# Moving the bit conversion of the second layer's weights between the experts of a mixture kernel

## The chip, the cores and the metric

The kernel runs on one core of one Trainium2 chip. The metric is the device time of one execution in microseconds (us); smaller is better. The kernel before takes 867.17 us, the median of three runs (866.35 to 868.37).

## The reference

Three stages run one after the other in one launch: attention over 4 batches, 8 heads, 512 local and 32 global positions; a mixture of eight experts in which every token goes to one expert; and a dense layer with a nonlinearity. Cut to the two later stages:

```python
def _moe_ref(x, w_gate, w1, w2):                # x: 2176 tokens x 512
    expert_idx = np.argmax(x @ w_gate, axis=1)
    gate_w = softmax(x @ w_gate)[np.arange(N), expert_idx]
    for e in range(8):
        mask = expert_idx == e
        h = np.maximum(x[mask] @ w1[e], 0.0)    # 512 -> 1024
        out[mask] = gate_w[mask, None] * (h @ w2[e])
def _moe2_ref(x, w_in, w_out):
    h = x @ w_in                                # 512 -> 2048, w_in and w_out are float64
    return (h - np.tanh(h)) @ w_out
```

## The kernel before

**Stages.** Attention and routing take the first 180 us or so. The experts follow, up to about 466 us, and the second layer after that.

**Experts.** Expert 0 comes first, the other seven in an order that the kernel finds from their token counts. The position in this order is called a place here, 0 to 7 (the variable `e` of `expert`, `expert_small`, `ahead`, the variable `p` of `CONV`). The places with more than 128 tokens (in this run 0, 1, 3, 5, 6 and 7) take the function `expert`, in which the tokens are the moving side of the matmuls; places 2 and 4 take `expert_small`. Each place has eight chunks `m` of 128 hidden units.

**Order in a place.** The schedule is written out by hand: each engine runs its instructions in the order of the program. For chunk m, `expert` emits the first matmuls `emit_L1(m)` (L1010, into the PSUM bank `pL1[m % 2]`), the two evictions of that bank (ACT's Relu L1013, DVE's low part L1014), the second matmuls `emit_L2(m - 2)` (L1021), and then `ahead(e, m)`. So TensorE's line reads L1(0), L1(1), L1(2), L2(0), L1(3), L2(1), ... L1(7), L2(5), L2(6), L2(7). A bank of `pL1` comes free when both evictions have read it: L1(m) waits for DVE's L1014 of chunk m - 2.

**What `ahead` emits.** First the split of a later chunk's weights into a high and a low part (ACT L935 twice, DVE L936, POOL L936), then the loads of raw weights on SP's queue (L120, L122), and then the conversion that this change is about.

**Conversion.** `w_in` and `w_out` arrive as float64. DVE builds the float32 bits from pairs of 32-bit words. There are 20 pieces q of 512 KB: 0 to 15 are the column blocks of `w_in`, 16 to 19 the first four row blocks of `w_out`. A piece at chunk m has its first two DVE operations (L946, L949, `pre_conv1`) at the end of `ahead(e, m)`; the third one (L952), ACT's rounding copy (L957), DVE's subtraction (L958) and the load of piece q + 2 (L965 or L968 on SP's queue, `pre_load`) follow in `ahead(e, m + 1)`, ahead of the first two operations of the next piece. The raw words lie in two buffers, `raw64[q % 2]`, so the load of piece q + 2 waits for L952 of piece q, and L946 of piece q waits for the load of piece q. The first two loads are issued ahead of place 0.

```python
        if (e, m - 1) in convs:
            pre_conv2(convs[e, m - 1], tmp64)   # L952, L957, L958, load of piece q + 2
        if (e, m) in convs:
            pre_conv1(convs[e, m], tmp64)       # L946, L949
```

`CONV` lists for each place the chunks that carry a piece, and `convs` numbers the pieces in that order. Before, place 0 has pieces 0, 1, 2 at chunks 0, 2, 4; place 1 has 3 to 9 at chunks 0 to 6; place 3 has 10 to 13 at 0, 1, 3, 4; places 5 and 7 have three each at 0, 2, 4.

Of the kernel before, what the change touches and what calls it, by code (L numbers as in the profile page):

```python
# [46 lines left out]
def body(ctx: ExitStack, tc: tile.TileContext, q_l, k_l, v_l, q_g, k_g, v_g,  # L47
# [980 lines left out]

    LS = 3

    CONV = ((0, 2, 4), (0, 1, 2, 3, 4, 5, 6), (), (0, 1, 3, 4), (), (0, 2, 4), (), (0, 2, 4))
    convs = {pm: q for q, pm in enumerate((p, m) for p in range(E) for m in CONV[p])}


# [440 lines left out]
```

## Time and profile before

| | |
|---|---|
| median of 3 runs | 867.17 us (866.35 to 868.37) |
| profiled execution | 869.88 us, its span 868.2 us |
| mean granted TensorE clock | 0.973 of full speed |
| TensorE (PE) busy | 801.0 us, 92% |
| VectorE (DVE) busy | 670.7 us, 77% |
| ScalarE (ACT) busy | 485.5 us, 56% |
| GpSimd (POOL) busy | 324.5 us, 37% |

The profile comes from one execution. Its own time is 1.68 us above its span (what lies around the first and the last instruction) and 2.71 us above the median of the runs. Times in rows count from the start of the span. In a row of the order in time the columns are start, duration, engine, line, operation, written tile, read tiles, shape and count; the brackets at the end give the idle time just ahead of it on its engine and what ended that. Matmul durations overlap their successors by about 0.16 us, so distances are better read from start to start.

### The profile page before, as it was taken

The numbers are of one execution on the slowest core, as the hardware profiler recorded it, in microseconds if no ns is written. First come the engines' busy times: TensorE is split into PE (matmuls) and PEld (weight loads), VectorE is DVE, ScalarE is ACT, GpSimd is POOL, SyncE is SP. The second block draws the span as 40 slices with busy tenths as digits, with TensorE's granted clock in tenths as the row PEclk, the third lists the DMA queues.
The fourth block names the chain that finished last, engine by engine and source line by source line (L and its number), as shares of the span: only waits on it lengthen the run. The fifth ranks groups of instructions, "written<-read, shape, count | busy, mean of one in ns | idle before, by whom it ended". The sixth has DMA issues, their size and how long they took to land. (4 is left out here: it accounts for less than half of the span.)

```text
span 868.2 us, 16570 instructions
## 1 busy us (share of the span) xinstructions
PE 801.0 (92%) x5456; PEld 698.1 (80%) x5456; DVE 670.7 (77%) x1430; ACT 485.5 (56%) x1179; POOL 324.5 (37%) x405
## 2 busy tenths in 40 slices
PE   8989999969899797787979988999999999999996
PEld 6767777758788687687979877789998999999885
DVE  6879999855468686776466999898698788778784
ACT  5777877634334443444535655575566565566564
POOL 7322253333212334333511566433433433343332
PEclk9999999979989899999989999999999999999999
DMA  6699974253856888798853223000000000010000
GB/s 147 140 251 225 279 195 148 91 192 97 266 168 197 204 237 255 180 264 281 213 130 103 83 91 109 25 24 26 25 22 27 13 35 19 1 44 1 12 26 25
DMA packets 145261, 105.71 MB, mean 122 GB/s; under 512 B 76608, under 2 KB 122176, under 8 KB 145088
## 3 DMA queue, kind: packets, MB, share of 16 engines
q1 hardware_dynamic: 142368, 94.83, 40.7%
q0 software_dynamic: 2720, 8.95, 2.7%
q8 instruction: 63, 1.03, 0.5%
q14 instruction: 110, 0.90, 0.4%
HBM read 78.75 MB, written 25.02 MB: 120 GB/s over the span
## 5 line engine op out<-in xcount | busy, mean ns | idle before, releaser
L1368 POOL TENSOR_TENSOR u<-u,z 128x384 f32<-128x384 f32 (+1 forms) x96 | 122.3, 1274 | 225.1 <-ACT u L1366 213.1
L936 POOL TENSOR_TENSOR w2s<-raw,w2s 128x512 fp32r<-128x512 f32 x64 | 90.4, 1420 | 192.7 <-ACT w2s L935 130.0
L1010 PE MATMUL pL<-xT,w1a 128*128 128x256 f32 (+4 forms) x588 | 110.4, 345 | 12.7 <-issue 4.8
L1010 PEld LDWEIGHTS pL<-xT,w1a 128*128 128x128 f32 x588 | 96.7, 209 | 22.9 <-issue 8.6
L1396 PE MATMUL pL<-wo,gT 128*128 128x512 f32 x417 | 108.9, 394 | 0.0
L1021 PE MATMUL pL<-hT,w2s 128*128 128x256 f32 (+4 forms) x576 | 98.2, 323 | 0.0
L1021 PEld LDWEIGHTS pL<-hT,w2s 128*128 128x128 f32 x576 | 87.2, 189 | 6.5
L1396 PEld LDWEIGHTS pL<-wo,gT 128*128 128x128 f32 x417 | 77.6, 188 | 14.3
L1383 DVE TENSOR_TENSOR gT<-g,gT 128x384 fp32r<-128x384 f32 (+1 forms) x64 | 80.5, 1258 | 0.7 <-ACT gT L1361 0.7
L936 DVE TENSOR_TENSOR w1a<-raw,w1a 128x512 fp32r<-128x512 f32 x64 | 62.6, 982 | 7.1 <-ACT w1a L935 4.2
L365 ACT ACTIVATE P<-sc,mx 128x224 f32<-128x224 f32 x128 | 60.6, 477 | 12.4 <-DVE mx L356 11.9
L1053 PE MATMUL pL<-xT,wih 128*128 128x384 f32 x256 | 65.3, 335 | 1.1 <-PEq L1282 1.1
L1373 DVE TENSOR_TENSOR g<-pL,z 128x384 f32<-128x384 f32 (+1 forms) x64 | 34.0, 531 | 41.5 <-ACT d L1356 41.5
L1355 ACT ACTIVATE z<-pL 128x384 f32<-128x384 f32 (+1 forms) x64 | 30.2, 471 | 61.9 <-PE pL L1053 59.7
L1053 PE MATMUL pL<-yB,wih 128*128 128x384 f32 (+1 forms) x256 | 59.5, 318 | 0.0
L1366 ACT ACTIVATE u<-z,c1t 128x384 f32<-128x384 f32 (+1 forms) x96 | 58.0, 605 | 0.0
L1367 ACT ACTIVATE mk<-z,nth 128x384 bf16<-128x384 f32 (+1 forms) x96 | 56.7, 590 | 0.0
L1379 DVE SCALAR_TENSOR_TENSOR g<-u,g 128x384 f32<-128x384 f32 (+1 forms) x96 | 55.1, 574 | 0.0
L1396 PE MATMUL pL<-wo,xT 128*128 128x512 f32 x207 | 54.5, 395 | 0.1
L1014 DVE SCALAR_TENSOR_TENSOR hT<-pL,hT 128x256 fp32r<-128x256 f32 (+4 forms) x48 | 24.9, 520 | 32.5 <-ACT hT L1013 32.4
L1053 PEld LDWEIGHTS pL<-xT,wih 128*128 128x128 f32 x256 | 46.7, 188 | 3.9 <-issue 1.4
L1361 ACT CAST gT<-g 128x384 fp32r<-128x384 f32 (+1 forms) x64 | 31.8, 496 | 31.8 <-DVE g L1387 31.8
(288 smaller groups left out, 1892.1 us busy)
## 6 DMA issues: line engine op xcount, KB each, us to landing
raw<-in_moe_w_dram SPq DMA_DIRECT2D x128, 256.0 KB, 6.0
xs<-zrow SPq DMA_DIRECT2D x32, 258.0 KB, 4.9
raw<-in_moe_w_in_dram SPq DMA_DIRECT2D x16, 512.0 KB, 5.2
raw<-in_moe_w_out_dram SPq DMA_DIRECT2D x16, 512.0 KB, 3.8
xrow<-xs SPq DMA_DIRECT2D x12, 516.0 KB, 5.7
yc<-yst SPq DMA_DIRECT2D x20, 256.0 KB, 5.7
nk<-in_k_l_dram SPq DMA_DIRECT2D x32, 128.0 KB, 3.7
nq<-in_q_l_dram SPq DMA_DIRECT2D x32, 128.0 KB, 3.4
```

Of the source, the lines that this page charges most:

```text
L365: nc.scalar.activation(out=P[:, j, 0:W], in_=sc[:, j], func=ACTF.Exp, scale=-1.0, bias=mx[:, j:j + 1], accum_out=sums[n][:, 2 * ip + j, h: ...
L936: (nc.gpsimd if lo else nc.vector).tensor_tensor(out=dl, in0=t[:, lo:lo + 512], in1=dh.bitcast(F32), op=ALU.subtract)
L1010: nc.tensor.matmul(ps[:, c], w1s[s][a][:, k], xT[x][:, k, c], start=a + x + k == 0, stop=x == 1 and k == KD - 1)
L1021: nc.tensor.matmul(pL2[j][:, 0:N], w2s[s][a][:, 128 * j:128 * (j + 1)], h[x][:, 0:N], start=st, stop=sp)
L1053: nc.tensor.matmul(ps[:, 0:n], a[:, m, k], y[x][:, k, 0:n], start=st, stop=sp)
L1366: nc.scalar.activation(out=u, in_=z, func=ACTF.Identity, scale=C2, bias=c1t)
L1367: nc.scalar.activation(out=mk, in_=z, func=ACTF.Relu, bias=nth)
L1368: nc.gpsimd.tensor_tensor(out=u, in0=u, in1=z, op=ALU.mult)
L1373: nc.vector.tensor_tensor(out=g, in0=h, in1=z, op=ALU.mult)
L1379: nc.vector.scalar_tensor_tensor(out=g, in0=u, scalar=C0, in1=g, op0=ALU.add, op1=ALU.mult)
L1383: nc.vector.tensor_tensor(out=t[1][:, 0:n], in0=g, in1=t[0][:, 0:n].bitcast(F32), op=ALU.subtract)
L1396: nc.tensor.matmul(p, g[a][:, 128 * j:128 * (j + 1)], w, start=st, stop=sp)
```

## The change

One table is changed. Place 0 gets pieces 0 to 6 at chunks 0 to 6, place 1 gets 7 to 13 at chunks 0 to 6, place 3 gets 14, 15 and 16 at chunks 1, 3 and 5, place 5 gets 17 and 18 at chunks 1 and 4, and place 7 gets 19 at chunk 2. The number of pieces is 20 in both.

```diff
-    CONV = ((0, 2, 4), (0, 1, 2, 3, 4, 5, 6), (), (0, 1, 3, 4), (), (0, 2, 4), (), (0, 2, 4))
+    CONV = (range(7), range(7), (), (1, 3, 5), (), (1, 4), (), (2,))
     convs = {pm: q for q, pm in enumerate((p, m) for p in range(E) for m in CONV[p])}
```

## Rows read from the trace of the kernel before

**Rows 1.** The page, its first part: busy time, share and instructions.

```profile
PE 801.0 (92%) x5456; PEld 698.1 (80%) x5456; DVE 670.7 (77%) x1430; ACT 485.5 (56%) x1179; POOL 324.5 (37%) x405
```

**Rows 2.** Busy time by stretch: length, engines, then clock, DMA share, GB/s. Places 0, 3.

```profile
core 0: us, PE busy (x) PEld busy (x) DVE busy (x) ACT busy (x) POOL busy (x), PEclk, DMA share, GB/s
189.50:233.50 44.00, 43.81 (x204) 38.22 (x204) 20.66 (x29) 15.59 (x29) 12.42 (x9) 0.96 0.62 179
...
312.00:347.50 35.50, 30.27 (x192) 29.42 (x192) 23.90 (x36) 14.69 (x31) 12.75 (x9) 0.95 0.78 235
```

**Rows 3.** Order in time on PE in place 0.

```profile
209.77 2.76 PE L1021 MATMUL pL<-hT,w2s 128*128 128x480 f32 x12
212.37 2.76 PE L1010 MATMUL pL<-xT,w1a 128*128 128x480 f32 x12
...
222.77 2.76 PE L1010 MATMUL pL<-xT,w1a 128*128 128x480 f32 x12
```

**Rows 4.** Order in time on DVE in place 0.

```profile
206.65 0.65 DVE L1014 SCALAR_TENSOR_TENSOR hT<-pL,hT 128x480 fp32r<-128x480 f32 x1
...
219.77 0.43 DVE L946 TENSOR_SCALAR tmp<-raw 128x512 int32<-128x512 int32 x1 [7.88 <-DMA raw<-in_moe_w_in_dram]
...
220.84 0.65 DVE L1014 SCALAR_TENSOR_TENSOR hT<-pL,hT 128x480 fp32r<-128x480 f32 x1
```

**Rows 5.** Order in time on SP's queue in place 0.

```profile
202.55 0.73 SPq L1224 DMA_DIRECT2D ids<-xs  x1
...
211.90 0.61 SPq L965 DMA_DIRECT2D raw<-in_moe_w_in_dram  x1
```

**Rows 6.** Line L965: issue to landing, first 205 to 220 us, then all.

```profile
DMA to landing us min/median/max: 7.2/7.5/7.8
...
DMA to landing us min/median/max: 4.5/5.2/8.9
```

**Rows 7.** Order in time in place 3, PE and DVE.

```profile
328.29 1.92 PE L1021 MATMUL pL<-hT,w2s 128*128 128x320 f32 x12
...
332.30 0.43 DVE L946 TENSOR_SCALAR tmp<-raw 128x512 int32<-128x512 int32 x1 [5.50 <-DMA raw<-in_moe_w_in_dram]
...
333.37 0.48 DVE L1014 SCALAR_TENSOR_TENSOR hT<-pL,hT 128x320 fp32r<-128x320 f32 x1
...
333.91 3.31 PE L1010 MATMUL pL<-xT,w1a 128*128 128x320 f32 x12 [3.69 <-DVE hT L1014]
...
337.06 1.92 PE L1021 MATMUL pL<-hT,w2s 128*128 128x320 f32 x12
```

**Rows 8.** The same on PE at the head of place 7, and its clock by stretch.

```profile
439.95 7.21 PE L1010 MATMUL pL<-xT,w1a 128*128 128x256 f32 x36 [3.89 <-issue]
446.99 1.60 PE L1021 MATMUL pL<-hT,w2s 128*128 128x256 f32 x12
...
440.00:445.00 5.00, 5.00 (x23) 5.00 (x24) 1.46 (x3) 0.38 (x1) 0.00 (x0) 0.50 0.57 103
```

**Rows 9.** Order in time in places 5 and 7, DVE and PE.

```profile
393.85 0.49 DVE L946 TENSOR_SCALAR tmp<-raw 128x512 int32<-128x512 int32 x1 [2.20 <-DMA raw<-in_moe_w_out_dram]
...
395.49 1.85 PE L1010 MATMUL pL<-xT,w1a 128*128 128x288 f32 x12 [0.74 <-DVE hT L1014]
...
454.65 1.70 PE L1010 MATMUL pL<-xT,w1a 128*128 128x256 f32 x12 [0.30 <-DVE hT L1014]
```

**Rows 10.** Order in time on DVE in place 1, evictions of chunks 3 and 7.

```profile
258.24 0.69 DVE L1014 SCALAR_TENSOR_TENSOR hT<-pL,hT 128x512 fp32r<-128x512 f32 x1
...
278.43 0.68 DVE L1014 SCALAR_TENSOR_TENSOR hT<-pL,hT 128x512 fp32r<-128x512 f32 x1
```

**Rows 11.** Order in time on PE behind places 3 and 5; a load in place 5.

```profile
347.55 0.87 PE L999 MATMUL pX<-idf,xrow 128*128 128x128 f32 x6 [1.53 <-issue]
...
397.12 0.37 SPq L968 DMA_DIRECT2D raw<-in_moe_w_out_dram  x1
...
405.55 1.97 PE L999 MATMUL pX<-idf,xrow 128*128 128x128 f32 x8 [3.48 <-issue]
```

## The prediction

> **What bounds the kernel now.** I read the page's busy times first: TensorE is busy 92% of the span, DVE 77% [rows 1]. So a change on DVE counts only where DVE makes TensorE wait. The busy time by stretch says where that can be: in place 0 TensorE works 43.81 of 44.00 us, in place 3 only 30.27 of 35.50 [rows 2]. Then I read the order in time on TensorE, DVE and SP's queue in both places, and looked in each for conversions that wait.
>
> In place 0 the matmul groups follow each other every 2.60 us; L1(5) starts at 212.37 and L1(7) at 222.77 [rows 3]. Yet DVE does wait there: the first operation of piece 2 (L946, chunk 4) sits idle 7.88 us until its load has landed, and starts at 219.77 [rows 4]. The wait is hidden, barely: the eviction behind it (L1014, chunk 5) ends at 220.84 + 0.65 = 221.49, and L1(7), which needs the bank, starts at 222.77, 1.3 us later. In place 3 the same wait, 5.50 us, is not hidden: L1014 ends at 333.37 + 0.48 = 333.85 and the next L1 group starts at 333.91 after an idle 3.69 us [rows 7]. That is the pattern to look for: a load lands late, L946 waits for it, the eviction behind L946 on DVE waits, and with it the bank of the L1 group two chunks on.
>
> **The change part by part.** In all, 20 pieces stay 20: the same operations and loads, in other chunks.
>
> *Place 0, the wait.* Piece 2 moves from chunk 4 to chunk 2. Its load is issued behind L952 of piece 0, which stays at chunk 1, so it stays where it is in SP's queue: issued at 211.90, behind the copy of row numbers of 202.55 and the loads of rows and raw weights [rows 5]. It took 7.87 us, to 219.77 [rows 4, 5]. So L946 of piece 2 now reaches the head of DVE's line right behind piece 1's subtraction, ahead of the eviction of chunk 3 (which ran at 206.65 [rows 4]), and cannot start before 219.77. Behind it on DVE are L949 and that eviction. By the distances of the rows the eviction ends 1.07 + 0.65 us after L946 starts, at 221.49. L1(5), which used that bank from 212.37 [rows 3], waits until then: 221.49 - 212.37 = +9.1 us. Bounds: the line's loads take 4.5 to 8.9 us to land, median 5.2 [rows 6]; landing at 217.1, the median, gives 6.4 us, landing at 220.8 gives 10.1. I take 9.1, because the two loads of that stretch took 7.2 and 7.8 [rows 6] and nothing issued ahead of it changes.
>
> The Trainium skill, page "DMA: Bandwidth & Descriptors", section "Queues, rings and completion order", says that each DMA engine takes the descriptors of a ring in order. By that rule what SP issues later cannot speed this load up, and the sum is the one I give; if the engines shared their time among all open transfers instead, the load could come down to its median and the sum would be 2.7 us lower.
>
> *Place 0, the clock.* After the idle time TensorE starts again at half its clock (1.2 of 2.4 GHz). In place 3, after 3.69 us idle, the group of twelve took 337.06 - 333.91 = 3.15 us where 1.92 - 0.16 = 1.76 is normal: +1.4 [rows 7]. At the head of place 7, after 3.89 us, 36 matmuls took 7.04 us where three groups of 1.44 are normal, +2.7, at a granted clock of 0.50 [rows 8]. I take +2.0, between the two.
>
> *Place 0, the rest.* Pieces 3 to 6 now follow chunk by chunk, as pieces 3 to 9 do in place 1, where DVE needs (278.43 - 258.24) / 4 = 5.05 us a chunk [rows 10]. From 220.84 the eviction of chunk 7 then comes at 241.0 and ends at 241.7. TensorE goes through seven groups from L1(5) to L2(6) by 221.5 + 7 x 2.60 + 2.0 = 241.7, and L2(7) needs that eviction. So DVE just keeps up: +0.5, with ends 0 and +3 (each of three loads a us later than DVE would want it). ACT's rounding copies stand ahead of the Relu of the next chunk, but that Relu has until L1(5) and is not late. On SP's queue the load of raw weights of chunk 3 waits for a split that DVE does after the wait, and the raw weights behind it come as much later. They belong to chunks of place 1; if that cover were gone, the delay of place 0 would reach place 1's splits.
>
> *Place 1* keeps seven pieces at the same chunks and loads that come as early: 0.
>
> *Place 3.* Pieces at chunks 1, 3 and 5 in place of 0, 1, 3 and 4. Pieces 14 and 15 were loaded in place 1, so the wait of 5.50 us goes. It is worth 333.91 - (328.29 + 1.76) = 3.9 us of idle and slow start of the group, and the 1.4 us of half clock: -5.25 [rows 7]. What is late next is the load of piece 16, issued in chunk 2 and wanted in chunk 5; the eviction behind it is that of chunk 6, which only L2(6) needs, three groups later. If it took the longest time of the line, 8.9 us [rows 6], it would cost up to 2 us; ends -3.3 and -5.25.
>
> *Place 5.* The wait for a `w_out` load at chunk 4 goes, 0.74 us of idle and 0.1 us of a slower group: -0.9 (-0.7 to -1.0) [rows 9]. *Place 7* keeps one piece, at chunk 2, and the 0.30 us of idle behind it [rows 9]; the two later ones slow their groups a little: -0.2 (0 to -0.8).
>
> *Ends of places.* Behind places 3 and 5 TensorE idles 1.53 and 3.48 us and the profile shows no releaser [rows 11]. The row of the load at 397.12 [rows 11] belongs to piece 18 and leaves place 5; a load of place 3 leaves as well. Whether these gaps hang on traffic the trace doesn't show; I take 0, with ends -3 and +2.
>
> **Sum.** 9.1 + 2.0 + 0.5 - 5.25 - 0.9 - 0.2 = +5.2 us. Against the profiled execution's own 869.88 us (span 868.2, 1.68 around it) that is 875.1. That execution stands 2.71 us above the median of the runs, 867.17, so the forecast for a run is 872.4.
>
> **The rivals.** *The transfers share the DMA engines* (ends faster). If open transfers slow each other rather than queue, the wait itself helps: while DVE waits, SP is held too, and the load lands after the shortest time of its line, 4.5 us [rows 6], at 216.4. The first term is then 5.7, the clock 1.4, the rest 0, and the lighter places 3 and 5 lose the idle 1.53 + 3.48 us [rows 11] and about 1 us of slow start behind it: 5.7 + 1.4 - 5.25 - 0.9 - 0.2 - 6.0 = -5.2, 861.9 us. It decides once it gives back over 5.2 us of what this sums up to. Against it: place 3's wait of 5.50 us held DVE in the same way, and did not shorten itself [rows 7]. Chance 0.10.
>
> *A shorter wait only.* The load lands at its median and the clock costs the lower end: 6.4 + 1.4 - 6.35 = +1.4, about 868.6: no change that can be told. Chance 0.13.
>
> *Every load of place 0 takes 7.5 us.* The two loads of the stretch did [rows 6]. Then each of pieces 4 to 6 waits again, the rest of place 0 costs its upper end, 3 us, and its end is late as places 3 and 5 are now, +2: 5.2 + 2.5 + 2 = +9.7, 876.9. For it: DVE has no spare time behind the first wait. Against it: SP is held during the wait, and the queue drains. Chance 0.15.
>
> *The pieces are no burden anywhere* (the change moves work that is hidden in both kernels): 867.2. Against it stands the idle of place 3, which is on the path [rows 7]. Chance 0.02.
>
> **How the numbers follow.** The forecast, 872.4, has 0.60. About 0.2%, 1.7 us, is what a measurement of this kernel tells from no change. Slower: 0.60 + 0.15 = 0.75; within: 0.13 + 0.02 = 0.15; faster: 0.10. All low ends of the terms together would be 864.9 and all high ends 881; they will not meet. The range leaves out the fast rival and the far end of the slow one: 867.0 to 878.0.
>
> **What would show it.** In the profile after: on DVE in place 0 one wait of L946 of 11 to 12 us, ending near 219.8, and behind it an idle of TensorE of about 9 us ahead of L1(5), put down to DVE's L1014; then a group at half clock; place 0 ending some 11 us later than 233.5. In place 3 no idle within the place, its length near 30 us in place of 35.5. The prediction is wrong if the load is issued well ahead of 211.9, if TensorE's idle in place 0 is under 6 us, or if the places behind give back more than 6.5 us.

## The result, and the profile after

| | before | after |
|---|---|---|
| median | 867.77 us (866.35 to 868.86) | 876.58 us (874.79 to 879.24) |
| profiled execution | 869.88 us | 879.24 us |
| mean granted clock | 0.973 | 0.967 |

The changed kernel is slower: 1.0105 of the time before, 95% interval [1.0072, 1.0138], some 8.8 us. The forecast was 872.4 us in a range of 867.0 to 878.0.

The page's busy times answer to [rows 1]. No engine has more work worth speaking of; the span is longer.

```profile
PE 803.3 (92%) x5456; PEld 699.9 (80%) x5456; DVE 668.5 (76%) x1430; ACT 486.5 (55%) x1179; POOL 325.4 (37%) x405
```

The stretches of places 0 and 3, and then three parts of place 0, in the columns of [rows 2]:

```profile
190.30:246.70 56.40, 46.28 (x204) 39.95 (x204) 30.67 (x45) 17.58 (x33) 12.48 (x9) 0.85 0.52 157
326.50:359.60 33.10, 28.98 (x192) 28.18 (x192) 21.52 (x32) 14.43 (x30) 12.48 (x9) 0.98 0.87 257
203.00:209.00 6.00, 6.00 (x29) 5.21 (x28) 4.67 (x7) 2.66 (x6) 1.49 (x1) 1.00 0.07 2
209.00:214.00 5.00, 4.14 (x20) 3.24 (x18) 0.69 (x1) 1.57 (x4) 1.29 (x1) 1.00 0.37 61
214.00:223.00 9.00, 0.00 (x0) 0.00 (x0) 1.50 (x3) 0.00 (x0) 0.00 (x0) 0.56 1.07 361
```

Place 0 grows from 44.00 to 56.40 us, and TensorE is idle for 10 of them, with its clock at 0.85 on the mean. The last three rows tell how the idle time comes about: up to 209 the DMA engines move next to nothing (2 GB/s), from 214 on they are full (361 GB/s), and no matmul runs in those 9 us.

Place 0 in order of time on TensorE, the answer to [rows 3]:

```profile
210.37 2.77 PE L1021 MATMUL pL<-hT,w2s 128*128 128x480 f32 x12
223.24 5.17 PE L1010 MATMUL pL<-xT,w1a 128*128 128x480 f32 x12 [10.10 <-DVE hT L1014]
228.21 3.02 PE L1021 MATMUL pL<-hT,w2s 128*128 128x480 f32 x12
...
252.15 0.33 PE L999 MATMUL pX<-idf,xrow 128*128 128x128 f32 x1 [2.82 <-issue]
```

On VectorE, the answer to [rows 4], and on SP's queue, the answer to [rows 5]:

```profile
209.11 0.69 DVE L958 TENSOR_TENSOR wil<-tmp,wih 128x512 fp32r<-128x512 f32 x1 [0.69 <-ACT wih L957]
221.46 0.43 DVE L946 TENSOR_SCALAR tmp<-raw 128x512 int32<-128x512 int32 x1 [11.66 <-DMA raw<-in_moe_w_in_dram]
...
222.53 0.65 DVE L1014 SCALAR_TENSOR_TENSOR hT<-pL,hT 128x480 fp32r<-128x480 f32 x1
```

```profile
203.87 0.73 SPq L1224 DMA_DIRECT2D ids<-xs  x1
206.41 0.40 SPq L120 DMA_DIRECT2D raw<-in_moe_w_dram  x1
207.07 2.40 SPq L122 DMA_DIRECT2D raw<-in_moe_w_dram  x1
...
214.27 0.38 SPq L965 DMA_DIRECT2D raw<-in_moe_w_in_dram  x1
```

The chain is the forecast one: the load of piece 2 is issued at 214.27 and lands 7.2 us later, L946 starts at 221.46 after a wait of 11.66 us, the eviction of chunk 3 (L1014) stands behind it and ends at 223.18, and L1(5) starts at 223.24. TensorE comes back at half its clock: the first group takes 228.21 - 223.24 = 4.97 us where 2.60 is normal, the next, which ends the low clock, 2.86 to the start of its successor at 231.07.

Place 3, the answer to [rows 7] and [rows 11]:

```profile
353.89 1.88 PE L1021 MATMUL pL<-hT,w2s 128*128 128x320 f32 x11 [0.19 <-DVE hT L1014]
359.66 1.54 PE L999 MATMUL pX<-idf,xrow 128*128 128x128 f32 x6 [3.89 <-DMA raw<-in_moe_w_dram]
...
363.16 4.18 PE L1133 MATMUL pL<-w1a,xT 128*128 128x256 f32 x18 [0.53 <-ACT xT L1001]
```

The wait inside place 3 is gone but for 0.19 us. The idle time behind it grew from 1.53 us [rows 11] to 3.89, and place 4 begins at the low clock: its 18 first matmuls take 4.18 us, 2.38 where the clock was full (row of the run e10 below).

The lengths of the eight places, from the first matmul L1 of one to that of the next (us, worked out from the starts of those groups on TensorE), for the kernels spoken of below. A comparison is one set of runs on one chip. The second, the third and the fifth comparison were on three different chips. Kernels are best compared within one: the kernel before took 871.98 us in the third and 866.41 in the fourth, which were the same chip.

| kernel | 0 | 1 | 2 | 3 | 4 | 5 | 6 | 7 |
|---|---|---|---|---|---|---|---|---|
| before | 49.25 | 51.99 | 21.21 | 40.15 | 21.52 | 35.44 | 30.87 | 26.57 |
| after | 62.97 | 51.81 | 21.46 | 36.60 | 23.00 | 33.77 | 31.14 | 24.65 |
| before, 2nd comparison | 48.30 | 48.14 | 21.87 | 42.36 | 21.01 | 36.63 | 33.07 | 26.07 |
| after, 2nd comparison | 63.64 | 51.71 | 20.25 | 36.51 | 22.64 | 34.44 | 31.85 | 25.84 |
| e5, 2nd comparison | 49.07 | 50.35 | 20.70 | 36.65 | 21.07 | 35.70 | 33.96 | 25.78 |
| e6, 2nd comparison | 53.68 | 51.85 | 20.69 | 37.09 | 21.72 | 35.12 | 30.99 | 26.03 |
| e1, 3rd comparison | 54.24 | 50.49 | 21.66 | 39.56 | 24.39 | 35.11 | 30.27 | 24.61 |
| e2, 3rd comparison | 58.14 | 51.97 | 21.39 | 38.79 | 21.35 | 35.04 | 30.78 | 25.25 |
| e3, 3rd comparison | 58.27 | 51.06 | 26.07 | 36.97 | 23.13 | 35.73 | 33.04 | 25.45 |
| e4, 3rd comparison | 63.12 | 51.94 | 20.43 | 38.98 | 21.10 | 33.48 | 31.75 | 25.75 |
| e9, 4th comparison | 51.07 | 53.27 | 22.39 | 35.51 | 19.91 | 33.54 | 31.34 | 24.61 |
| e10, 4th comparison | 50.36 | 50.80 | 20.44 | 35.98 | 20.23 | 34.59 | 30.93 | 25.78 |
| e11, 4th comparison | 48.73 | 49.05 | 20.47 | 35.43 | 21.02 | 34.97 | 31.21 | 25.34 |
| e12, 5th comparison | 56.86 | 53.32 | 21.31 | 36.08 | 21.02 | 32.73 | 31.10 | 25.45 |

Of before to after, place 0 costs +13.7 us and the places behind it give back 5.7 (3: -3.55, 4: +1.48, 5: -1.67, 7: -1.92).

A length includes the gap behind the place, in which the next tokens are transposed. Without it, from its first group to the end of its last, place 0 takes 43.8 and 43.4 us in the two executions of the kernel before, 56.5 and 56.4 after, 51.1 in e2, 46.6 in e6, 49.5 in e1, 52.2 in e3, 50.5 in e12, and 43.6 in e9, e10 and e11. These are the steadier numbers: the gap behind place 0 lies between 4.8 and 7.4 us, and the first 36 matmuls of place 1 take 8.3 to 11.2 us.

### The profile page after: what moved, and what is told of

It is laid out like the page before. It is cut to its first block, busy times and chain, and to the rows that moved or that the text cites. A ratio compares the mean times of both kernels' runs of the same rounds, so it can differ in the third digit from the quotient of the medians.

```text
span 877.5 us, 16563 instructions
## 1 busy us (share of the span) xinstructions
PE 803.3 (92%) x5456; PEld 699.9 (80%) x5456; DVE 668.5 (76%) x1430; ACT 486.5 (55%) x1179; POOL 325.4 (37%) x405
## 5 line engine op out<-in xcount | busy, mean ns | idle before, releaser
L936 POOL TENSOR_TENSOR w2s<-raw,w2s 128x512 fp32r<-128x512 f32 x64 | 90.9, 1424 | 199.0 <-ACT w2s L935 152.0
L1010 PE MATMUL pL<-xT,w1a 128*128 128x256 f32 (+4 forms) x588 | 108.8, 339 | 19.6 <-DVE hT L1014 10.1
L1010 PEld LDWEIGHTS pL<-xT,w1a 128*128 128x128 f32 x588 | 94.3, 203 | 29.9 <-DVE hT L1014 10.5
L1021 PE MATMUL pL<-hT,w2s 128*128 128x256 f32 (+4 forms) x576 | 98.7, 323 | 0.2 <-DVE hT L1014 0.2
L1021 PEld LDWEIGHTS pL<-hT,w2s 128*128 128x128 f32 x576 | 87.6, 190 | 7.1 <-DVE hT L1014 0.4
L365 ACT ACTIVATE P<-sc,mx 128x224 f32<-128x224 f32 x128 | 60.6, 477 | 11.7 <-DVE mx L356 11.2
L936 DVE TENSOR_TENSOR w1a<-raw,w1a 128x512 fp32r<-128x512 f32 x64 | 61.8, 967 | 4.7 <-ACT w1a L935 3.7
L1014 DVE SCALAR_TENSOR_TENSOR hT<-pL,hT 128x256 fp32r<-128x256 f32 (+4 forms) x48 | 25.0, 521 | 42.3 <-ACT hT L1013 39.4
L1013 ACT ACTIVATE hT<-pL 128x256 fp32r<-128x256 f32 (+4 forms) x48 | 22.2, 463 | 50.5 <-PE pL L1010 50.4
```

The costliest lines, as they stand in the source:

```text
L365: nc.scalar.activation(out=P[:, j, 0:W], in_=sc[:, j], func=ACTF.Exp, scale=-1.0, bias=mx[:, j:j + 1], accum_out=sums[n][:, 2 * ip + j, h: ...
L936: (nc.gpsimd if lo else nc.vector).tensor_tensor(out=dl, in0=t[:, lo:lo + 512], in1=dh.bitcast(F32), op=ALU.subtract)
L1010: nc.tensor.matmul(ps[:, c], w1s[s][a][:, k], xT[x][:, k, c], start=a + x + k == 0, stop=x == 1 and k == KD - 1)
L1021: nc.tensor.matmul(pL2[j][:, 0:N], w2s[s][a][:, 128 * j:128 * (j + 1)], h[x][:, 0:N], start=st, stop=sp)
```

## The experiments

Theory 1 is the prediction's: place 0 waits for the load of piece 2, which is issued too late, and seven pieces are no burden by their work. Theory 2 says that seven pieces are too much work for VectorE. The quoted passages are what was expected ahead of each run; times in them are those of the first comparison, so they are judged here by the ratio to the kernel before. The theory that the loads are late because they stand behind other transfers came in as the runs went on. Before takes part in every comparison.

### The changed kernel (e7) and the kernel before (e8), once more

Both were run again, with no edit, in the second comparison.

> The kernel before, once more, on the chip of the three runs beside it: its trace gives place lengths that can be compared within one chip. Ratio 1.000; place 0 near 49 us, place 3 with an idle of 3 to 4 us behind a late load. If the idle of place 3 is much smaller here, what the later places can give back is smaller too.

> The changed kernel on the same chip as its variants. Ratio to before 1.008 to 1.013; place 0 near 63 us with an idle of 10 us ahead of L1(5).

Before: 870.56 us, ratio 0.9998 [0.9977, 1.002]. After: 878.31 us, ratio 1.0093 [1.0071, 1.0116]. The wait in place 0 of the changed kernel, on TensorE:

```profile
223.23 5.17 PE L1010 MATMUL pL<-xT,w1a 128*128 128x480 f32 x12 [9.69 <-DVE hT L1014]
```

The loss and its place are those of the first comparison, and so is the idle time inside place 3 of the kernel before (3.90 us there). Place 1 of the kernel before differs: 48.14 us here, 51.99 in the first comparison. 2.7 us of that are its first 36 matmuls, 8.30 us at a granted clock of 1.00 here and 11.01 there, which begin at 0.50.

### One chunk later for piece 2 (e2)

```diff
-    CONV = (range(7), range(7), (), (1, 3, 5), (), (1, 4), (), (2,))
+    CONV = ((0, 1, 3, 4, 5, 6), range(7), (), (1, 3, 5), (), (1, 4), (), (2, 4))
```

> The changed kernel with piece 2 a chunk later (place 0 at chunks 0, 1, 3, 4, 5, 6) and the seventh piece at chunk 4 of place 7. The load is issued at the same point. Theory 1: it lands at the same time, near 221, but now ahead of the eviction of chunk 4, which L1(6) needs 5.2 us later than L1(5): TensorE's idle shrinks from 10.1 by 5.2 to about 4.9 us, ahead of L1(6) and not of L1(5); half clock still costs some 2 us; about 876.6 - 5 = 871.5 us. Theory 2: one piece less saves about one chunk's conversion on DVE, 3 us at most, and the place of the idle is not tied to chunk 4.

876.72 us, ratio 1.0055 [1.0032, 1.0077]. The wait on VectorE and the idle time on TensorE:

```profile
221.49 0.43 DVE L946 TENSOR_SCALAR tmp<-raw 128x512 int32<-128x512 int32 x1 [10.45 <-DMA raw<-in_moe_w_in_dram]
```

```profile
223.26 3.17 PE L1010 MATMUL pL<-xT,w1a 128*128 128x480 f32 x7 [4.64 <-DVE hT L1014]
```

(The second row ends with its window; the whole group of twelve takes 4.81 us to the start of the next.) The load lands at the same time, and the group that waits for it is the next L1 group, L1(6). One chunk is two groups, 5.2 us; the idle time falls by 5.46. The wait decides, not the number of pieces.

### Two pieces less around the late load (e6)

```diff
+    CONV = ((0, 1, 4, 5, 6), range(7), (), (1, 3, 5), (), (1, 4), (), (2, 4, 6))
```

> Place 0 with five pieces, at chunks 0, 1, 4, 5, 6: piece 2 is at chunk 4 as in the kernel before, pieces 3 and 4 behind it; place 1 seven, place 3 at 1, 3, 5, place 5 at 1, 4, place 7 at 2, 4, 6. Theory 1 (the wait for the load of piece 2 and who stands behind it): no idle of TensorE of over 1 us in place 0, place 0 near 50 us; the time stands by the later places alone, 0.993 to 1.001 of before. Theory 2 (too many pieces on DVE in place 0): five pieces in place of three cost about two fifths of what seven cost, 1.003 to 1.006.

873.13 us, ratio 1.004 [1.0024, 1.0056]. With piece 2 at chunk 4 as in the kernel before, no group waits for it any more. On TensorE:

```profile
232.48 2.65 PE L1021 MATMUL pL<-hT,w2s 128*128 128x480 f32 x11 [2.21 <-DVE hT L1014]
236.44 1.10 PE L999 MATMUL pX<-idf,xrow 128*128 128x128 f32 x8 [1.32 <-issue]
...
241.06 0.47 PE L999 MATMUL pX<-idf,xrow 128*128 128x128 f32 x1 [1.94 <-issue]
```

Place 0 is shorter by 10 us than in the kernel after, yet 5.4 longer than before on that chip: the load of piece 4 is late by 1.06 us, the conversion then runs at a third of its speed (1.35 us for 0.43) and L2(7) waits 2.21; and the end of the place idles 1.32 and 1.94 us, with no releaser. Theory 1 alone gave too little here, and the ratio lies where theory 2 had it (1.003 to 1.006); but it is again a late load that starts the wait, and e10 below tells the two theories apart.

### Pieces 2 and 3 loaded ahead of place 0 (e1)

```diff
+    yst2 = [mc.tile([128, 1024], F32, name=f"yst{j}") for j in range(2)]
+    yst = [yst2[j // 2][:, 512 * (j % 2):512 * (j % 2 + 1)] for j in range(4)]
...
+    def raw_of(q):
+        return yst2[q % 2].bitcast(I32) if q in (2, 3) else raw64[q % 2]
...
-        pre_load(q + 2)
+        if q not in (2, 3):
+            pre_load(q + (4 if q < 2 else 2))
...
+    pre_load(2)
+    pre_load(3)
```

> The changed kernel, all 20 pieces at the same chunks; only pieces 2 and 3 are read into a buffer of their own (the staging tiles of the results, free until the end of place 0), with loads issued ahead of place 0. Theory 1 (DVE waits for the load of piece 2, and TensorE behind it for a bank): the wait of 11.66 us of L946 goes, piece 4 waits instead at chunk 4, hidden as in the kernel before; TensorE's idle of 10.10 us ahead of L1(5) goes, and with it the group at half clock (2.4 us): 876.6 - 10.3 - 2.6 = 863.7 us, 862 to 867. Theory 2 (seven pieces are simply too much for DVE in place 0, the load only shows where it waits): TensorE idles elsewhere in place 0 for most of the same time; 871 us or more.

873.22 us beside 871.98, ratio 1.0011 [0.9991, 1.0032]: the loss is gone within the interval, but the gain that was expected does not come. On VectorE and TensorE (lines stand 1 and 5 higher in this kernel: L947 is L946, L1015 and L1026 are L1010 and L1021):

```profile
221.68 0.43 DVE L947 TENSOR_SCALAR tmp<-raw 128x512 int32<-128x512 int32 x1 [2.85 <-DMA raw<-in_moe_w_in_dram]
...
231.97 1.27 DVE L947 TENSOR_SCALAR tmp<-raw 128x512 int32<-128x512 int32 x1 [1.11 <-DMA raw<-in_moe_w_in_dram]
```

```profile
223.46 2.87 PE L1015 MATMUL pL<-xT,w1a 128*128 128x480 f32 x12 [0.52 <-DVE hT L1019]
...
234.59 4.77 PE L1026 MATMUL pL<-hT,w2s 128*128 128x480 f32 x11 [2.85 <-DVE hT L1019]
```

The idle time of 10 us is gone with the late load of piece 2: that part of the theory is shown. Now pieces 4 and 6 are late; theory 1 had said so of piece 4 only, and as hidden. Between first and last group place 0 is still 5.7 us longer than in the kernel before.

### The copy of row numbers (e3 and e12)

Ahead of the load of piece 2 in SP's queue stands the copy of place 0's row numbers (L1224), 2 KB in words of four bytes, which takes 8.4 us to land in the kernel after. First the copies of all places were moved behind their place, then that of place 0 alone.

```diff
     for e in range(E):
-        put_ids(xos[e], yos[e])
...
         place(e)
+        put_ids(xos[e], yos[e])
```

> The changed kernel with the copy of row numbers (L1224, 512 rows of 4 bytes) issued behind each place instead of ahead of it. It tests why the load takes 7.1 us: the DMA engines move next to nothing from 204 to 213 us, behind that copy. If the copy stands at the head of the queue and holds what follows: the load lands some 4.5 to 5.2 us after its issue and the loads ahead of it are issued faster; TensorE's idle ahead of L1(5) falls from 10.1 to 3 to 7 us, and the starts of the other large places have less to wait for; 868 to 873 us. If the slow start has another reason: idle and time as in the changed kernel, 876.6 us.

880.56 us beside 871.98, ratio 1.0096 [1.0064, 1.0128], the same as without the edit. Idle time ahead of L1(5) falls to 5.87 us as expected, but what that saves is lost elsewhere: within place 2 and at the end of place 6 stand gaps of 4.48 and 5.38 us with no releaser. Which of the eight moves did that isn't told apart, so the second form:

```diff
+        if e:
             put_ids(xos[e], yos[e])
...
         place(e)
+        if e == 0:
+            put_ids(xos[e], yos[e])
```

> The kernel after with only one thing moved: the copy of row numbers of place 0 goes behind that place on SP's queue; all other copies stay. Theory A (of the wait in place 0, about 4 us is the copy ahead of the load in the queue, the rest is that the load is issued only behind the third operation of piece 0): the idle of TensorE ahead of L1(5) is 5 to 7 us instead of 10, the load of piece 2 lands near 216 to 218, the end of place 0 keeps its waits, place 0 takes 57 to 59 us, later places as in the kernel after, ratio 1.004 to 1.007. Theory C (the copy is no part of it; in the run with all copies moved the load was only issued earlier): the idle stays at 9 to 10 us and the ratio at 1.009 to 1.011.

871.19 us beside 864.97, ratio 1.0074 [1.0049, 1.0099]. SP's queue, TensorE, and the stretches of place 0:

```profile
205.99 0.39 SPq L120 DMA_DIRECT2D raw<-in_moe_w_dram  x1
206.66 0.33 SPq L122 DMA_DIRECT2D raw<-in_moe_w_dram  x1
...
210.47 0.53 SPq L965 DMA_DIRECT2D raw<-in_moe_w_in_dram  x1
```

```profile
218.98 4.43 PE L1010 MATMUL pL<-xT,w1a 128*128 128x480 f32 x12 [4.43 <-DVE hT L1014]
```

```profile
203.00:209.00 6.00, 6.00 (x30) 5.19 (x29) 5.16 (x8) 2.12 (x4) 1.50 (x1) 1.00 0.30 92
209.00:214.00 5.00, 5.00 (x25) 4.34 (x24) 1.51 (x3) 2.12 (x4) 1.28 (x1) 1.00 0.92 296
```

Without the copy at the head the loads behind it move at once: 92 GB/s instead of 2 from 203 to 209, 296 instead of 61 after that. The first L120 takes 3.0 us to land, where behind the copy it took 8.6. L122, whose issue took 2.40 us in the kernel after, takes 0.33, so that the load of piece 2 is issued 210.47 - 191.08 = 19.4 us after the start of the place instead of 23.95, and the idle time is 4.43 us instead of 10.10. The load lands 5.0 us earlier, 26.1 instead of 31.1 us after the start of the place: so much of the wait is the copy. The other 0.7 us of the shorter idle time is TensorE coming later to L1(5), after a slower start of the place (granted clock 0.77 from 190 to 203 us, 0.87 in the kernel after). From its issue to its landing the load itself still takes 6.7 us, at full engines.

Two things remain in SP's queue. The load is not issued as soon as the third operation of piece 0 (L952) is done, as theory A had it: that ends at 203.56 in the kernel after and at 204.94 in e12, 10.7 and 5.5 us ahead of the issue; the load stands behind other transfers. And SP issues no transfer at all from 192.8 us to the copy at 203.87 (to 205.99 in e12). What holds it there the profile doesn't show, and no run took it apart.

In the times the saving is smaller (the ratio falls from 1.0105 and 1.0093 to 1.0074, just above what was expected); part of it the intervals allow, and what became of the rest is open.

### Both together (e9)

The early loads, and the copy of place 0 behind it: the two edits above in one kernel.

> The kernel after with the loads of pieces 2 and 3 issued ahead of place 0, into the tiles that later hold the experts' results, and the copy of row numbers of place 0 moved behind that place on SP's queue. In the earlier run with the early loads alone, pieces 4 and 6 still waited for their loads (0.52 and 2.85 us of TensorE idle). Theory A: those loads are late because they stand behind the copy of row numbers on SP's queue; then both idles vanish, place 0 takes 49 to 50 us instead of 54.2, and the ratio to the kernel before is 0.993 to 0.997. Theory B: they are late because place 0 moves too many bytes in too short a time; then an idle of 2 to 3 us ahead of a late group of place 0 stays, place 0 takes 53 to 55 us, and the ratio is about 1.001.

866.69 us beside 866.41, ratio 1.0007 [0.9987, 1.0027], the ratio that theory B gave. TensorE at the end of place 0:

```profile
223.74 2.76 PE L1015 MATMUL pL<-xT,w1a 128*128 128x480 f32 x12
226.34 7.96 PE L1026 MATMUL pL<-hT,w2s 128*128 128x480 f32 x36
235.72 1.09 PE L1004 MATMUL pX<-idf,xrow 128*128 128x128 f32 x8 [1.42 <-issue]
...
241.73 10.79 PE L1015 MATMUL pL<-xT,w1a 128*128 128x512 f32 x36 [0.56 <-issue]
```

Within place 0 theory A holds: with seven pieces in it and all their loads, the groups follow each other every 2.60 us without a gap to the last chunk; the load of piece 6 alone is 0.22 us late, without effect. From first to last group the place takes 43.6 us, as in the kernel before. The total did not follow it. The gap behind the place is 7.4 us long, 5.2 in e11 on the same chip, and place 1 starts at the low clock (granted 0.53 over its first 5.3 us): its first 36 matmuls take 10.6 us, 8.3 in e11. The kernels before and after start place 1 that way too (11.0 and 11.2 us in the first comparison), so the low clock alone doesn't set e9 apart.

### The same work without the loads (e10)

The loads of pieces 2 to 6 are left out; these pieces convert the words of pieces 0 and 1 again.

```diff
-        if q >= M2 + PW:
+        if q >= M2 + PW or 2 <= q <= 6:
             return
         t = raw64[q % 2]
```

> The kernel after without the loads of pieces 2 to 6: these pieces convert the words of pieces 0 and 1 that lie in the two buffers, so that a part of w_in is left out. VectorE, ScalarE and GpSimd do the same work as in the kernel after; only 2.5 MB of transfers and the waits for them are gone. Theory 1 (the loads are what place 0 waits for): no idle in place 0, its length about 49 us as in the kernel before, the gains of places 3, 5 and 7 stay, ratio 0.993 to 0.995. Theory 2 (seven pieces are too much work for VectorE beside the evictions, whatever the loads): TensorE still idles 3 us or more in the second half of place 0, its length stays at 53 us or more, ratio 0.998 or more.

864.77 us beside 866.41, ratio 0.998 [0.9953, 1.0006]. On VectorE the evictions of chunks 6 and 7, on TensorE the last groups of place 0 and the first group of place 4:

```profile
228.66 0.65 DVE L1014 SCALAR_TENSOR_TENSOR hT<-pL,hT 128x480 fp32r<-128x480 f32 x1
...
233.53 0.65 DVE L1014 SCALAR_TENSOR_TENSOR hT<-pL,hT 128x480 fp32r<-128x480 f32 x1
```

```profile
226.72 2.76 PE L1010 MATMUL pL<-xT,w1a 128*128 128x480 f32 x12
229.32 7.97 PE L1021 MATMUL pL<-hT,w2s 128*128 128x480 f32 x36
238.28 1.09 PE L999 MATMUL pX<-idf,xrow 128*128 128x128 f32 x8 [0.99 <-issue]
...
351.25 2.38 PE L1133 MATMUL pL<-w1a,xT 128*128 128x256 f32 x18 [1.62 <-ACT yst L1026]
```

Theory 2 falls: VectorE does all seven pieces at 4.87 us a chunk, TensorE needs 5.20, and no group of place 0 waits. What place 0 lost to the change it lost to transfers and the waits for them. The gain in the total (1.6 us) is smaller than the 4 to 6 expected, and its interval reaches up to no gain at all.

### Place 3 as before (e4), and places 0 and 1 as before (e5, e11)

Place 3 given back its pieces of chunks 0, 1, 3 and 4, with the change kept in places 0 and 1:

```diff
+    CONV = (range(7), range(7), (), (0, 1, 3, 4), (), (0, 2), (), ())
```

> The changed kernel's first two places (seven pieces each), with the six others where the kernel before had its first six later ones: place 3 at chunks 0, 1, 3, 4 and place 5 at 0, 2. It measures what the sparser later places gave back. The load for chunk 3 of place 3 is again issued in chunk 1 of that place, so theory 1 expects the wait of L946 of some 5 us, an idle of TensorE near 3.7 us and the half clock in place 3 back, on top of place 0's loss: 876.6 + 5 = 881 to 882 us. If the later places gave back nothing, 876.6 us.

880.51 us beside 871.98, ratio 1.0092 [1.0063, 1.0121]: the loss of 5 us over the kernel after (1.0105 and 1.0093) that theory 1 expected can't be measured. On TensorE in place 3:

```profile
349.91 2.58 PE L1010 MATMUL pL<-xT,w1a 128*128 128x320 f32 x12 [2.34 <-DVE hT L1014]
352.29 2.94 PE L1021 MATMUL pL<-hT,w2s 128*128 128x320 f32 x12
...
364.18 1.00 PE L999 MATMUL pX<-idf,xrow 128*128 128x128 f32 x6 [1.91 <-DMA raw<-in_moe_w_dram]
```

The wait inside the place is back (2.34 us, and 1.6 us of slow matmuls), and from first to last group place 3 is 3.7 us longer. But the idle time behind the place is 1.91 us instead of 3.89 and place 4 is 1.9 us shorter. By the lengths, places 3 to 7 together are 1.9 us longer than in the first execution of the kernel after and 0.2 shorter than in the second.

The other way round (e5): place 0 as before, places 3 and 5 as in the change, three pieces in place 6 and two in place 7.

```diff
+    CONV = ((0, 2, 4), range(7), (), (1, 3, 5), (), (1, 4), (1, 3, 5), (2, 4))
```

> The first two places as in the kernel before (three and seven pieces), the other ten spread thinner: place 3 at chunks 1, 3, 5, place 5 at 1, 4, place 6 at 1, 3, 5, place 7 at 2, 4. It measures the other half of the change by itself. If the late loads of places 3, 5 and 7 are worth what the rows of before said (6 us) and nothing takes their place: 0.993 of before, 5 to 6 us faster. If the time saved within these places returns at their ends (the next tokens' transposes wait there for code while weights are loading): 0.998 to 1.001.

868.14 us beside 870.0, ratio 0.9968 [0.9949, 0.9987]: faster than both kernels, by about half of the 5 to 6 us that would have come if nothing took the place of the late loads. Place 3 takes 36.65 us instead of 42.36 on that chip. Place 6 pays for its three pieces: 27.8 us from first to last group, 24.9 in the kernel before on that chip, of which the length shows only 0.9, because the gap behind place 6 was 8.2 us there and 6.1 here. On VectorE:

```profile
410.41 1.54 DVE L946 TENSOR_SCALAR tmp<-raw 128x512 int32<-128x512 int32 x1
411.98 1.66 DVE L949 SCALAR_TENSOR_TENSOR tmp<-raw,tmp 128x512 int32<-128x512 int32 x1
```

The two operations take 3.2 us where they take 1.1 in place 0; GpSimd's split (L936) runs from 410.37 to 413.10 beside them. Spread more thinly (e11):

```diff
+    CONV = ((0, 2, 4), range(7), (), (1, 3, 5), (), (1, 3, 5), (1, 4), (1, 4))
```

> Three pieces in place 0 and seven in place 1 as in the kernel before; the other ten as 3, 3, 2 and 2 in places 3, 5, 6 and 7 instead of 4, 3, 0 and 3. If the loads are hidden wherever the pieces stand two chunks apart, place 3 loses its inner idle (length 37 instead of 40 to 42 us), places 5 and 6 keep the length of the kernel before within 0.7 us, and the ratio is 0.993 to 0.997, at or below the 0.9968 of the run with 3, 2, 3 and 2. If a piece costs its work in any place, place 6 takes 0.6 us more than before and the ratio is 0.997 to 1.000.

862.89 us beside 866.41, ratio 0.9961 [0.9941, 0.998], the best of all, though not told apart from e5. On TensorE in place 6 no group waits any more (24.2 us from first to last); its last groups:

```profile
421.89 1.60 PE L1010 MATMUL pL<-xT,w1a 128*128 128x256 f32 x12
423.33 4.48 PE L1021 MATMUL pL<-hT,w2s 128*128 128x256 f32 x36
```

## Why the prediction was right, and what it mis-sized

Slower was forecast, and the mechanism is the one forecast: late load, L946 ahead of the eviction, bank of L1(5). e2 moves the wait by a chunk and takes 5.5 us off it, e1 takes it away, e10 shows that the work alone makes no group of place 0 wait. The size, +5.2 us, was 3.6 short of the medians. By the profiled executions (+9.36) the terms stand so, with the gap behind a place counted from the end of its last group to the first group of the next:

- *The wait*, forecast +9.1: L1(5) would have started at 210.37 + 2.60 = 212.97 and started at 223.24, +10.3, beyond the upper bound of 10.1 by a little. The step that was off is "it stays where it is in SP's queue: issued at 211.90". It stayed in its place in the order, but it came 23.95 us after the start of the place instead of 22.38. The copy of row numbers came 0.5 us later (13.55 for 13.03), and the L122 straight ahead of the load took 2.11 us to issue instead of 1.08 (rows below); the 2.40 us of the L122 behind the copy are not new, they were 2.36. The 7.2 us from issue to landing were in the bounds.
- *The clock*, forecast +2.0: (4.97 - 2.60) + (2.86 - 2.60) = +2.6, near the upper end.
- *The rest of place 0*, forecast +0.5 with VectorE at 5.05 us a chunk: the period was 4.87 to 4.94 and no further load was waited for. What is left inside place 0 is -0.2.
- *Ends of places*, forecast 0 with ends -3 and +2: behind place 0 +1.0, behind place 5 -0.7, and place 4, which starts at the low clock, +1.5 by its length. Behind place 3 it is +1.3: the idle time ahead of the transposes is 2.4 us longer, and from there to place 4's first group it takes 1.1 less. In all +3.1, beyond the upper end. This is the term that was worst. It had been set at 0 for want of a releaser, where the idle times of 1.53 and 3.48 us [rows 11] said that something there is waited for.
- *Place 3*, forecast -5.25: -4.8 from first to last group. *Place 5*: forecast -0.9, -1.0. *Place 7*: forecast -0.2 and at most -0.8; -1.9, of which 1.1 is a faster head (its first 36 matmuls take 6.09 us, 7.21 in [rows 8]). With the gaps behind them and place 4 the later places give back 5.7, forecast 6.35. Places 1, 2 and 6 (+0.3 together), the later start of place 0 (190.32 for 189.52) and about 0.1 behind the places make up the 9.36.

SP's queue in the kernel before, first, and in the kernel after, last:

```profile
205.77 2.36 SPq L122 DMA_DIRECT2D raw<-in_moe_w_dram  x1
210.72 1.08 SPq L122 DMA_DIRECT2D raw<-in_moe_w_dram  x1
...
212.06 2.11 SPq L122 DMA_DIRECT2D raw<-in_moe_w_dram  x1
```

That the time stayed in the range is luck in part. The median stood 1.4 us below the upper end, and place 7 gave 1.7 us more than forecast, for the most part by its head at a higher granted clock (0.75 for 0.57); with place 7 as forecast the time would have been some 878.3, an estimate. Of the signs named, the wait of L946 and the idle time ahead of L1(5) came; the length of 30 us for place 3 did not, it was 33.1 by the same stretch, with the longer idle time at its end.

Of the rivals, "every load of place 0 takes 7.5 us" had nearly the time that came (876.9) but not by its way: pieces 3 to 6 did not wait in the kernel after; only its late end of the place was there. In e1, with the first wait gone, pieces 4 and 6 did wait, which fits the prediction's reason against this rival, that the queue drains during the first wait. "The transfers share the DMA engines" wanted the load to land 4.5 us after its issue while SP is held; it took 7.2. In the kernel after this load of 512 KB, issued at 214.27, landed at 221.4, and the two loads of 256 KB issued 0.6 and 1.3 us behind it landed at 222.2 and 222.9, in the order of issue though they are half as large. The Trainium skill (page "DMA: Bandwidth & Descriptors", section "Queues, rings and completion order") says that a DMA engine takes the descriptors of a ring in order. These landings agree with it. e12 speaks for what stands ahead in the queue rather than for the sharing of engines: of the 5.0 us by which its landing came forward, 4.6 are an earlier issue. "A shorter wait only" and "the pieces are no burden anywhere" gave less than came.

What the prediction had not seen at all is why the load is late: it took the copy of row numbers as one transfer among others ahead of it [rows 5]. By e12 the copy makes 5.0 us of the wait (by e3, in which the start of L1(5) came forward from 32.9 to 28.7 us after the start of the place, 4.2). The kernel before has the same copy and the same held queue (10 GB/s from 203 to 209 us); there piece 2 was wanted two chunks later, and the wait was hidden.

Open: the ends of places. The idle times there have no releaser or a weight load as a releaser, and their change went against the expectation in e4 and was not foreseen in e3 and e9. A hint lies in the DMA queues of the changed kernel, first the 8 us from 246 on (the end of place 0), then 8 us within place 1, packets, megabytes and the share of 16 engines' time:

```profile
q1 hardware_dynamic: 1390, 1.38, 60.6%
q14 instruction: 7, 0.06, 2.0%
...
q1 hardware_dynamic: 1200, 1.05, 45.1%
```

In the first stretch instructions are fetched (queue 14), in the second none, and the fetches share the engines with the weights, which reached 360 to 400 GB/s in parts of the first. No run took that apart, so it stays a guess that TensorE waits for its code.

## What to carry to other kernels

Before moving a step that waits for a load, follow the load back through its queue to what holds its issue, and read the DMA rate of the stretch: a stretch at 2 GB/s with loads already issued is a held queue, not spare room. An idle time without a releaser at the end of a stage shouldn't be set at zero when the change alters the traffic there. Where work is to be spread, thinly and with room ahead of each load (e11) beat bringing it forward.

## What the runs showed of the hardware that was not expected

- A copy of 2 KB in words of four bytes took 8.4 us to land and held up 256 KB loads issued 2.5 and 3.2 us behind it on the same queue: the first took 8.6 us to land with the copy ahead, 3.0 without, and the engines moved 2 GB/s from 203 to 209 us with it, 92 without (after and e12).
- The same conversion operation (L946) takes 0.43 us alone and 1.27 to 1.54 us where it runs beside a split on GpSimd for most of its time (e1, e5, e6). In the 14 traces every L946 of over 0.9 us overlaps a GpSimd split, and the short ones overlap one by 0.5 us at most.
- After 10.1 us of idle time TensorE lost 2.6 us (granted clock 0.50 over the first group); after 4.64 us in e2 it lost 2.2 (0.52); after 4.43 us in e12 1.6 (0.60; 218.98 to the next group at 223.22, 4.24 for 2.60); after 2.85 us in e1 2.2 (0.50); after 2.34 us in e4 1.6 (0.76, then 0.59); after 2.21 us in e6 nothing that shows (1.00). The loss does not follow the length of the gap.
- The start of place 0 lay between 188.5 and 193.9 us in kernels that leave everything ahead of it alone but for a load or two: a scatter of up to 5 us that no comparison of single executions sees through.
